# Causal attention and a gated expert layer on one core: port waits for GpSimd, a store moved ahead of a load, and new numbers in the planner

## The chip, the cores and the metric

The kernel runs on one core of a Trainium2 chip. The metric is the device time of one execution in microseconds (us). The kernel before was timed in three runs: 681.15, 683.09 and 684.12 us, median 683.09.

## What is computed

Four batches of twelve heads go through causal attention (448 tokens, head width 64); the heads' outputs are joined to a matrix x of 1792 tokens by 768, and x goes through a gated layer with float32 weights.

```python
scores = scale * np.matmul(q, k.transpose(0, 1, 3, 2))
scores = np.where(mask, -1000000000.0, scores)
scores = scores - np.max(scores, axis=-1, keepdims=True)
attn = np.exp(scores)
attn = attn / (np.sum(attn, axis=-1, keepdims=True) + 1e-09)
attn_out = np.matmul(attn, v)
...
x = np.ascontiguousarray(attn_out.transpose(0, 2, 1, 3)).reshape(B * S, H * D)
g = x @ w_gate
silu = g * (1.0 / (1.0 + np.exp(-g)))
val = x @ w_val
return (silu * val @ w_out)
```

## The kernel before, in words

**Stages.** One chunk is one batch, 448 tokens. For each chunk the kernel does the attention of six pairs of heads, and then the layer: 36 weight tiles of 128x768 (24 of gate and value, 12 of the output matrix). A float32 product is made of three matmuls on high and low parts (`mm3`, L885 to L887): 2592 matmuls of 128x448 in all, with `M` (gate and value) and `MO` (output) as their names in the rows. Attention runs one chunk ahead: while TensorE multiplies the weights of chunk c, the other engines make chunk c+1's scores (`S`, L512), row maxima (L563), exponentials (L575), normalised rows (L620 on ScalarE, L624 on GpSimd), transposes (`T`, L678 and L710) and products with the values (`O`, L752 and L783). So every stage fills TensorE with two kinds of work.

**Weights.** In chunk 0 a weight arrives as 64-bit numbers, 768 KB (`wide`, three buffers, load at L859). A copy takes the upper part into the single tile `top` (ScalarE, L317, or GpSimd, L323), a VectorE instruction joins it with the lower bits into float32 (`wraw`, two buffers, L868), and two more instructions split `wraw` into a high and a low part (`whl`, L317, L323, L339 or L342). `wraw` is also stored to HBM (`wr`, 384 KB, L832, the function `keep`), so that chunk 1 can load it back. A `wraw` buffer is free again when its split is done and its store has landed. In chunk 1 the split parts are stored (`ws`), and chunks 2 and 3 load them.

**Order.** A planner written in the kernel sets the order of everything. Each operation has costs per engine (`cost`, L65), a due time, dependencies and buffers; `Planner.run` gives out operations in time order, lets operations that can run on several engines choose one, and returns one list. The program is then written out in this list's order, and each engine runs its own instructions in that order. The planner knows that VectorE and GpSimd share a port to the on-chip memory: an operation marked `port` on VectorE and any operation on GpSimd never overlap in the plan (`lock`, `begin`). In the program nothing holds them to that: an engine starts an instruction when its semaphores allow it. All loads and stores go through one queue, issued by SyncE (SP) in plan order; a DMA whose semaphore is not there yet holds up all that are behind it.

**End.** The output tile of the last `MO` is scaled and moved to on-chip memory in two halves, 256 columns by ScalarE (L954) and 192 by VectorE (L955), each with a store of its own (L962). All other output tiles are one instruction of 448 columns and one store (L974).

Of the kernel before, what the change touches and what calls it, by code (L numbers as in the profile page):

```python
# [8 lines left out]
F32 = mybir.dt.float32  # L9
# [5 lines left out]
AF = mybir.ActivationFunctionType  # L15
ALU = mybir.AluOpType

P = 128
# [45 lines left out]

def cost(e, kind, n):  # L65
    if e == "ACT":
        return {"psum": 66, "sbuf": 110, "ptr": 190, "exp": 280, "tanh": 160}[kind] / 1e3 + n / 1200
    if e == "DVE":
        return 0.075 + n / {"one": 1920}.get(kind, 960)
    if e == "POOL":  # L70
        return {"one": 190, "ptr": 260, "two": 180}[kind] / 1e3 + n / {"two": 465.0}.get(kind, 1200.0)
    return {"r": max(n * 0.4475e-3 + 0.0025, 0.109), "f": n * 0.4475e-3 + 0.0045, "n": n / 600, "t": n * 0.109 / 128}[kind] + 0.001


class Res:
# [154 lines left out]
def kernel(  # L230
# [25 lines left out]
    def buf(shape, dt, tag, base, name):  # L256
        return pool.tile(shape, dt, tag=tag, name=name, bufs=CAPS[base])
# [46 lines left out]
    def op(alts, due, deps=(), alloc=(), uses=(), extra=0.0):  # L304
        first = [heads[r.tag] for r in alloc if r.tag in heads]
        o = pl_.op(alts, due, list(deps) + first, alloc, uses, extra)
        o.soft = first
        o.port = bool(alts.pop("port", False))
        o.kb = alts.pop("kb", 0)
        o.kind = alts.pop("kind", "m")  # L310
        for r in alloc:
            heads[r.tag] = o
        return o

    def copies(kind, n, out, in_, scale=1.0, engines="ADP"):
        def act():
            nc.scalar.activation(out(), in_(), AF.Copy, scale=scale)  # L317

        def dve():
            nc.vector.tensor_scalar(out(), in_(), scale, None, ALU.mult)  # L320

        def gps():
            nc.gpsimd.tensor_scalar(out(), in_(), scale, 1.0, ALU.mult, ALU.mult)  # L323

        r = {}
        if "A" in engines:
            r["ACT"] = (cost("ACT", kind, n), act)
        if "D" in engines:
            r["DVE"] = (cost("DVE", "one" if kind == "sbuf" else "two", n), dve)
        if kind == "sbuf":  # L330
            r["port"] = True
        if "P" in engines and kind == "sbuf":
            r["POOL"] = (cost("POOL", "one", n), gps)
        return r

# [476 lines left out]
    def weights(i):  # L812
        c, g = seq[i]
        due = start[c + 1] + LEN[c + 1] * g / NW
        w = wt[i] = {}
        rhl = Res("whl")

        def newhl():
            w["hl"] = buf([P, 2, WC], F32R, "whl", "whl", f"whl{i}")
            w["h"], w["l"] = w["hl"][:, 0], w["hl"][:, 1]  # L820

        def split(ra, rw):
            def newh():
                newhl()
                return w["h"]
            h = op(copies("sbuf", WC, newh, lambda: w["raw"]), due - 6 * WLEAD, [ra], [rhl], [rw])
            l = op(binary(WC, lambda: w["l"], lambda: w["raw"], lambda: raw(w["h"])), due - 5 * WLEAD, [h], [], [rw, rhl])
            wops[i] = (h, l, rhl, rhl)
            return h, l

        def keep(dst, src, deps, use, kb):
            return op({"SP": (0.3, lambda: nc.sync.dma_start(dst, src())), "kb": kb}, due - 3 * WLEAD, deps, [], [use])  # L832

        if c and (g, "hl") in stored:
            def load():
                newhl()
                nc.sync.dma_start(raw(w["hl"]), scratch[g])
            ld = op({"SP": (0.3, load), "kb": 768}, due - 10 * WLEAD, [stored[g, "hl"]], [rhl])
            wops[i] = (ld, ld, rhl, rhl)
            return  # L840
        if c:
            rw = Res("wraw")

            def load():
                w["raw"] = buf([P, WC], F32, "wraw", "wraw", f"wraw{i}")
                nc.sync.dma_start(w["raw"], scratch1[g])
            ld = op({"SP": (0.3, load), "kb": 384}, due - 12 * WLEAD, [stored[g, "raw"]], [rw])
            h, l = split(ld, rw)
            if c in RAW and c < NCHUNK - 1:
                stored[g, "hl"] = keep(scratch[g], lambda: raw(w["hl"]), [h, l], rhl, 768)  # L850
            return

        rw, r64, rt_ = Res("wraw"), Res("wide"), Res("top")

        def load():
            w["wide"] = buf([P, 4 * WC + 4], U16, "wide", "wide", f"wide{i}")
            nc.sync.dma_start(w["wide"][:, 1 : 4 * WC + 1], wP[g].bitcast(U16))  # L859
        ld = op({"SP": (0.3, load), "kb": 768}, due - 16 * WLEAD, alloc=[r64])  # L860

        def upper():
            return top.bitcast(F16).rearrange("p (n w) -> p n w", w=2)[:, :, 1]

        def lower():
            w["raw"] = buf([P, WC], F32, "wraw", "wraw", f"wraw{i}")
            z = w["wide"].bitcast(U32).rearrange("p (n w) -> p n w", w=2)[:, :WC, 1]
            nc.vector.scalar_tensor_tensor(w["raw"].bitcast(U32), z, 13, top, ALU.logical_shift_right, ALU.bitwise_or)  # L868

        bf = lambda: w["wide"].bitcast(BF16).rearrange("p (n w) -> p n w", w=4)[:, 1 : WC + 1, 0]  # L870
        g0 = op(copies("sbuf", WC, upper, bf), due - 10 * WLEAD, [ld], [rt_], [r64])
        ra = op({"DVE": (cost("DVE", "two", WC), lower), "port": True}, due - 8.5 * WLEAD, [g0], [rw], [r64, rt_])

        h, l = split(ra, rw)
        if 0 in RAW:
            stored[g, "hl"] = keep(scratch[g], lambda: raw(w["hl"]), [h, l], rhl, 768)
        else:
            stored[g, "raw"] = keep(scratch1[g], lambda: w["raw"], [ra], rw, 384)

    ps = {}  # L880

# [7 lines left out]
    def moe(c):  # L889
# [45 lines left out]
        for m in range(KD):  # L935
            rM = Res("M")
            prev = None
            for f in range(NF):
                half, kb = divmod(f, KD)
                gi = 2 * NF + 2 * m + half  # L940
                i = base + gi
                wh_, wl_, rwh, rwl = wops[i]
                a, l, rhh, rhl = h_ops[f]

                def mm(f=f, kb=kb, i=i, m=m):
                    if f == 0:
                        ps[c, "o", m] = bank("M", f"MO{c}_{m}")
                    mm3(ps[c, "o", m], i, kb, N, hh[f][:, :N], hl[f][:, :N], f == 0, f == NF - 1)
                prev = op({"PE": (m3, mm)}, at(gi + kb / KD), [prev, wh_, wl_, a, l],
                          [rM] if f == 0 else [], [rwh, rwl, rhh, rhl] + ([rM] if f else []))  # L950
            if (c, m) == (NCHUNK - 1, KD - 1):

                cut = 256
                for name, eng, put, a, b_ in (("ACT", nc.scalar, lambda o, i_: nc.scalar.activation(o, i_, AF.Copy, scale=0.5), 0, cut),  # L954
                                              ("DVE", nc.sync, lambda o, i_: nc.vector.tensor_scalar(o, i_, 0.5, None, ALU.mult), cut, N)):  # L955
                    ro = Res("osb")

                    def half(m=m, put=put, a=a, b_=b_):
                        o = ps[c, "s", m, a] = buf([P, T], F32, "osb", "osb", f"osb{c}_{m}_{a}")[:, a:b_]
                        put(o, ps[c, "o", m][:, a:b_])  # L960
                    e = op({name: (0.4, half)}, at(gi + 1) - BOOST, [prev], [ro], [rM])
                    op({"SP": (0.3, lambda m=m, eng=eng, a=a, b_=b_: eng.dma_start(  # L962
                        outT[m * P : (m + 1) * P, TO[c] + a : TO[c] + b_], ps[c, "s", m, a])), "kb": 112}, at(gi + 1), [e], [], [ro])
                continue
            ro = Res("osb")

            def newo(m=m):
                ps[c, "s", m] = buf([P, T], F32, "osb", "osb", f"osb{c}_{m}")[:, :N]
                return ps[c, "s", m]
            e = op(copies("psum", N, newo, lambda m=m: ps[c, "o", m][:, :N], 0.5, engines="AD"),  # L970
                   at(gi + 1) - BOOST, [prev], [ro], [rM])

            def store(m=m):
                nc.sync.dma_start(outT[m * P : (m + 1) * P, TO[c] : TO[c] + N], ps[c, "s", m])  # L974
            op({"SP": (0.3, store), "kb": 224}, at(gi + 1), [e], [], [ro])
# [3 lines left out]
    for c in range(NCHUNK):  # L979
# [4 lines left out]
            split_x(c, k)  # L984
        moe(c)
    order = pl_.run(CAPS)
    with tc.manual_schedule():
        for o in order:
            o.fn()


# [49 lines left out]
```

## Time and profile before

| | |
|---|---|
| runs | 681.15, 683.09, 684.12 us |
| profiled execution | 680.74 us; first to last instruction 678.9 us |
| TensorE busy | 667.2 us, 98% |
| VectorE busy | 378.3 us, 56% |
| ScalarE busy | 360.1 us, 53% |
| GpSimd busy | 218.5 us, 32% |
| DMA | 165.08 MB, 243 GB/s |

Busy time of TensorE is the union of its matmuls' modelled spans, which overlap; what it leaves is time in which no matmul ran. The granted clock was full in all 40 slices of the page.

### The profile page before, as it was taken

The numbers are of one execution on the slowest core, as the hardware profiler recorded it, in microseconds if no ns is written. First come the engines' busy times: TensorE is split into PE (matmuls) and PEld (weight loads), VectorE is DVE, ScalarE is ACT, GpSimd is POOL, SyncE is SP. The second block draws the span as 40 slices with busy tenths as digits, with TensorE's granted clock in tenths as the row PEclk, the third lists the DMA queues.
The fourth block names the chain that finished last, engine by engine and source line by source line (L and its number), as shares of the span: only waits on it lengthen the run. The fifth ranks groups of instructions, "written<-read, shape, count | busy, mean of one in ns | idle before, by whom it ended". The sixth has DMA issues, their size and how long they took to land.

```text
span 678.9 us, 10972 instructions
## 1 busy us (share of the span) xinstructions
PE 667.2 (98%) x3906; PEld 600.7 (88%) x3906; DVE 378.3 (56%) x926; ACT 360.1 (53%) x875; POOL 218.5 (32%) x256
## 2 busy tenths in 40 slices
PE   8999999999999999999999999999999999999997
PEld 5568899888999999999899999999999999999997
DVE  6778879797785676676765346545534222222100
ACT  7997688688683765654755345346354211111000
POOL 3773645456361342554423224224232000000000
PEclk9999999999999999999999999999999999999999
DMA  8868787878987978878688975554565666666671
GB/s 296 292 182 272 244 270 248 301 236 293 289 287 251 307 280 296 277 255 306 227 315 298 340 253 186 199 187 144 182 200 179 218 226 212 217 225 224 220 248 42
DMA packets 45446, 165.08 MB, mean 243 GB/s; under 512 B 5072, under 2 KB 14672, under 8 KB 45392
## 3 DMA queue, kind: packets, MB, share of 16 engines
q1 hardware_dynamic: 45088, 164.16, 72.2%
q8 instruction: 31, 0.51, 0.3%
q10 hardware_dynamic: 304, 0.23, 0.1%
q14 instruction: 23, 0.19, 0.1%
HBM read 116.39 MB, written 47.97 MB: 242 GB/s over the span
## 4 chain that ended last, share of the span: by engine, by line
PE 80%; DVE 6%; ACT 5%; DMA 5%; issue 2%; SPq 1%; POOL 1%; DVEq 0%; ACTq 0%; POOLq 0%
PE M L885 14%; PE M L886 14%; PE M L887 14%; PE MO L886 8%; PE MO L885 8%; PE MO L887 8%; PE S L512 5%; PE O L752 4%; DMA wr<-wraw 4%; PE T L710 4%; DVE wraw L868 3%; ACT p L575 2%; ACT p L620 1%; PE T L678 1%; PE O L783 1%
## 5 line engine op out<-in xcount | busy, mean ns | idle before, releaser
L885 PE MATMUL M<-xh,whl 128*128 128x448 f32 x576 | 215.4, 374 | 0.0
L886 PE MATMUL M<-xl,whl 128*128 128x448 f32 x576 | 209.4, 364 | 0.0
L887 PE MATMUL M<-xh,whl 128*128 128x448 f32 x576 | 209.1, 363 | 0.0
L887 PEld LDWEIGHTS M<-xh,whl 128*128 128x128 f32 x576 | 108.0, 188 | 7.7
L885 PEld LDWEIGHTS M<-xh,whl 128*128 128x128 f32 x576 | 108.2, 188 | 7.3 <-issue 0.3
L886 PEld LDWEIGHTS M<-xl,whl 128*128 128x128 f32 x576 | 108.4, 188 | 6.7 <-DVE xl L339 0.3
L885 PE MATMUL MO<-hh,whl 128*128 128x448 f32 x288 | 107.1, 372 | 0.0
L886 PE MATMUL MO<-hl,whl 128*128 128x448 f32 x288 | 104.6, 363 | 0.0
L887 PE MATMUL MO<-hh,whl 128*128 128x448 f32 x288 | 104.5, 363 | 0.0
L575 ACT ACTIVATE p<-p,m 128x192 f32<-128x192 f32 (+3 forms) x180 | 91.5, 513 | 3.3 <-DVE m L563 3.2
L563 DVE CUSTOM_DVE_ANT_0 p<-S,masks 128x192 f32<-128x192 f32 (+3 forms) x180 | 68.1, 426 | 16.9 <-PE S L512 16.4
L317 ACT ACTIVATE ph<-T 128x384 fp32r<-128x384 f32 (+3 forms) x95 | 47.5, 510 | 53.1 <-PE T L678 27.8
L339 DVE TENSOR_TENSOR whl<-wraw,whl 128x768 fp32r<-128x768 f32 x58 | 55.8, 962 | 10.0 <-ACT whl L317 8.0
L620 ACT ACTIVATE p<-p,rec 128x448 f32<-128x448 f32 (+3 forms) x130 | 58.7, 512 | 5.0 <-DVE rec L588 4.9
L317 ACT ACTIVATE hh<-t 128x448 fp32r<-128x448 f32 x42 | 24.1, 575 | 67.4 <-DVE t L928 67.4
L922 DVE SCALAR_TENSOR_TENSOR t<-t,M 128x448 f32<-128x448 f32 x48 | 29.7, 618 | 52.4 <-ACT t L918 52.3
L887 PEld LDWEIGHTS MO<-hh,whl 128*128 128x128 f32 x288 | 54.0, 188 | 3.8
L885 PEld LDWEIGHTS MO<-hh,whl 128*128 128x128 f32 x288 | 54.2, 188 | 3.4
L886 PEld LDWEIGHTS MO<-hl,whl 128*128 128x128 f32 x288 | 54.2, 188 | 3.2
L928 DVE TENSOR_TENSOR t<-t,M 128x448 f32<-128x448 f32 x48 | 29.6, 616 | 43.8 <-PE M L887 43.3
L339 DVE TENSOR_TENSOR pl<-T,ph 128x384 fp32r<-128x384 f32 x72 | 39.6, 549 | 23.0 <-ACT ph L317 22.7
L918 ACT ACTIVATE t<-M 128x448 f32<-128x448 f32 x48 | 26.0, 542 | 49.1 <-PE M L887 48.8
(82 smaller groups left out, 887.8 us busy)
## 6 DMA issues: line engine op xcount, KB each, us to landing
whl<-ws SPq DMA_DIRECT2D x72, 768.0 KB, 4.3
wide<-in_w_dram SPq DMA_DIRECT2D x36, 768.0 KB, 5.4
ws<-whl SPq DMA_DIRECT2D x36, 768.0 KB, 4.2
wr<-wraw SPq DMA_DIRECT2D x36, 384.0 KB, 5.9
wraw<-wr SPq DMA_DIRECT2D x36, 384.0 KB, 5.0
vraw<-in_v_dram SPq DMA_DIRECT2D x24, 256.0 KB, 4.4
qraw<-in_q_dram SPq DMA_DIRECT2D x23, 224.0 KB, 4.0
kraw<-in_k_dram SPq DMA_DIRECT2D x23, 224.0 KB, 4.7
```

Source lines behind the costliest of these rows:

```text
L317: nc.scalar.activation(out(), in_(), AF.Copy, scale=scale)
L339: r["DVE"] = (cost("DVE", "two", n), lambda: nc.vector.tensor_tensor(out(), a(), b(), alu))
L512: nc.tensor.matmul(st[u + y][f"S{i}"][:r], Q[:, q0 : q0 + r], K[:, :q1_] if y else K[:, S - q1_ :], start=z == 0, stop=z == len(passes) - 1)
L563: nc.vector.tensor_tensor_reduce(p[:r], s[f"S{i}"][:r], mask[:r, maskX - q0 : maskX - q0 + q1_] if h % 2 else back[:r, P - min(q1_, P) : P ...
L575: nc.scalar.activation(p[:r], p[:r], AF.Exp, bias=peak(i)[:r], scale=-1.0, accum_out=sums[u % NR][:r, i : i + 1],)
L620: nc.scalar.activation(p[:r], p[:r], AF.Copy, scale=rec[u % NR][:r, i : i + 1])
L710: nc.tensor.transpose(pt[:, o_ + q0 - bs : o_ + q0 - bs + r], s[f"p{i}"][:r, k0 : k0 + P], ident[:r, :r])
L885: nc.tensor.matmul(out[:, :n], a[:, w], xhi, start=first, stop=False)
L886: nc.tensor.matmul(out[:, :n], a[:, w], xlo, start=False, stop=False)
L887: nc.tensor.matmul(out[:, :n], l[:, w], xhi, start=False, stop=last)
L922: nc.vector.scalar_tensor_tensor(t, t, 1.0, ps[c, f, 0][:, :N], ALU.add, ALU.mult)
L928: nc.vector.tensor_tensor(t, t, ps[c, f, 1][:, :N], ALU.mult)
```

## The change

Five edits. (1) The planner's costs: the copy of `top` gets a kind of its own, `half`, with 340 instead of 110 ns of fixed cost on ScalarE, and a high-precision matmul loses some ns. (2) The store of `wraw` becomes due 17 instead of 3 units ahead of its weight's use, which is one unit ahead of a load. (3) The last output tile is no longer cut in two. (4) While the program is written out, the last VectorE operation marked `port` is kept; a GpSimd operation that comes after it in the plan, and starts there less than 4 us behind its end, gets a semaphore wait for it. (5) With the new costs the plan comes out in another order.

```diff
-        return {"psum": 66, "sbuf": 110, "ptr": 190, "exp": 280, "tanh": 160}[kind] / 1e3 + n / 1200
+        return {"psum": 66, "sbuf": 110, "half": 340, "ptr": 190, "exp": 280, "tanh": 160}[kind] / 1e3 + n / 1200
...
-    return {"r": max(n * 0.4475e-3 + 0.0025, 0.109), "f": n * 0.4475e-3 + 0.0045, "n": n / 600, "t": n * 0.109 / 128}[kind] + 0.001
+    return {"r": max(n * 0.4445e-3, 0.109), "f": n * 0.4475e-3 + 0.0045, "n": n / 600, "t": n * 0.109 / 128}[kind] + 0.001
...
-        def keep(dst, src, deps, use, kb):
-            return op({"SP": (0.3, lambda: nc.sync.dma_start(dst, src())), "kb": kb}, due - 3 * WLEAD, deps, [], [use])
+        def keep(dst, src, deps, use, kb, lead=3):
+            return op({"SP": (0.3, lambda: nc.sync.dma_start(dst, src())), "kb": kb}, due - lead * WLEAD, deps, [], [use])
...
-        g0 = op(copies("sbuf", WC, upper, bf), due - 10 * WLEAD, [ld], [rt_], [r64])
+        g0 = op(copies("half", WC, upper, bf), due - 10 * WLEAD, [ld], [rt_], [r64])
...
-            stored[g, "raw"] = keep(scratch1[g], lambda: w["raw"], [ra], rw, 384)
+            stored[g, "raw"] = keep(scratch1[g], lambda: w["raw"], [ra], rw, 384, 17)
...
-            if (c, m) == (NCHUNK - 1, KD - 1):
-
-                cut = 256
...
-                continue
...
+    after = mybir.DependencyInfo(mybir.DependencyClass.Sync, mybir.DependencyReason.DATA)
     with tc.manual_schedule():
+        port = None
         for o in order:
+            made = nc.cur_bb.bb.instructions
+            n = len(made)
             o.fn()
+            mine = [i for i in nc.cur_bb.bb.instructions[n:] if i.engine == {"DVE": nc.vector, "POOL": nc.gpsimd}.get(o.eng, nc.sync).engine]
+            if o.eng == "DVE" and o.port:
+                port = (o, mine[-1])
+            if o.eng == "POOL" and port and o.start - port[0].end < 4 and port[0] not in o.deps:
+
+                tc.add_manual_dep(mine[0], port[1].name, after, reason="port")
```

**The order it moves.** On SyncE's queue, in chunk 0's weights (the number behind `wide` and `wr` is the weight):

```order
-L859 DMA wide5_790<-in_w_dram 128x3072
 L832 DMA wr2_193<-wraw2_771 128x768
+L859 DMA wide5_791<-in_w_dram 128x3072
 L422 DMA vraw14_841<-in_v_dram 128x512
-L859 DMA wide6_858<-in_w_dram 128x3072
 L832 DMA wr3_194<-wraw3_847 128x768
-L859 DMA wide7_912<-in_w_dram 128x3072
+L859 DMA wide6_865<-in_w_dram 128x3072
 L832 DMA wr4_195<-wraw4_907 128x768
```

The load of weight 5 stood ahead of the store of weight 2 and now stands behind it; this pair, store of weight i and load of weight i+3, is turned round for all the weights of chunk 0 that have such a load.

On GpSimd, before, around the low part of weight 21 (`whl`, L342; `VS`, `QS` and `p` belong to attention, `hl` is the low part of a hidden tile):

```order
L323 TENSOR_SCALAR VS_1947<-vraw_1288 128x4x64 [waits DMAHW3_49,PE_49]
L342 TENSOR_TENSOR QS_1890<-qraw_1004,QS_1890 128x448 [waits DMAHW1_49,Activation_49]
L624 TENSOR_SCALAR p_3_1935<-p_3_1935,rec 128x448 [waits DVE_49,Activation_49]
L342 TENSOR_TENSOR VS_1947<-vraw_1288,VS_1947 128x4x64 [waits Pool_49]
L342 TENSOR_TENSOR whl_1913<-wraw_1888,whl_1913 128x768
L342 TENSOR_TENSOR hl_110<-t_9_1960,hh_98 128x448 [waits Activation_49]
```

and with the change:

```order
L342 TENSOR_TENSOR QS_1888<-qraw_1007,QS_1888 128x448 [waits DMAHW1_49,Activation_49]
L624 TENSOR_SCALAR p_0_1462<-p_0_1462,rec 64x64 [waits DVE_49,Activation_49]
L624 TENSOR_SCALAR p_2_1931<-p_2_1931,rec 128x320 [waits Activation_49]
L342 TENSOR_TENSOR KS_1902<-kraw_1033,KS_1902 128x448 [waits DMAHW2_49]
L342 TENSOR_TENSOR whl_1913<-wraw_1886,whl_1913 128x768 [waits DVE_49,Pool_49]
L323 TENSOR_SCALAR top<-wide_1905 128x768 [waits DMAHW1_49,DVE_49,Activation_49]
```

The same low part had no wait and followed its neighbour at once; now it waits for VectorE. Over the whole program GpSimd's rows that wait for VectorE go from 68 to 116. TensorE has the same 3764 rows, in the same order up to about its 297th, which is in the first products of chunk 0.

At the end, on ScalarE (`osb` is an output tile on its way out):

```order
-L954 ACTIVATE osb_5_0_7224<-MO_5_7184 128x256 [waits DMAHW1_49,PE_49,Activation_49]
-L962 DMA out_dram<-osb_5_0_7224 128x256 [waits DMAHW3_49,Activation_49]
-L1037 UNCONDITIONAL_BRANCH
+L317 ACTIVATE osb_5_7224<-MO_5_7184 128x448 [waits DMAHW1_49,PE_49,Activation_49]
+L1033 UNCONDITIONAL_BRANCH
```

One instruction of ScalarE takes the place of two halves, and one store of SyncE that of two.

## Rows read from the trace of the kernel before

**Rows 1.** The page: span and busy time of the engines.

```profile
span 678.9 us, 10972 instructions
PE 667.2 (98%) x3906; PEld 600.7 (88%) x3906; DVE 378.3 (56%) x926; ACT 360.1 (53%) x875; POOL 218.5 (32%) x256
```

**Rows 2.** Busy time by stretch: stretch, length, engines (x instructions), clock, DMA share, GB/s.

```profile
10.00:50.00 40.00, 38.46 (x280) 23.78 (x276) 31.45 (x113) 39.52 (x121) 26.79 (x31) 1.00 0.80 268
50.00:100.00 50.00, 49.09 (x298) 43.36 (x299) 40.71 (x88) 38.55 (x85) 27.04 (x25) 1.00 0.83 267
100.00:160.00 60.00, 57.35 (x336) 51.40 (x335) 52.20 (x102) 47.78 (x99) 29.75 (x30) 1.00 0.83 265
...
280.00:340.00 60.00, 59.47 (x351) 54.65 (x350) 41.48 (x95) 36.99 (x91) 25.25 (x27) 1.00 0.79 270
```

**Rows 3.** Timeline of TensorE: start, length, what [idle before, who ended it].

```profile
50.13 0.44 PE L678 MATMUL T<-ident,p 128*128 128x128 f32 x2 [0.73 <-POOL p L624]
...
75.49 0.65 PE L752 MATMUL O<-ph,VS 128*128 128x448 f32 x3 [0.56 <-DVE ph L339]
...
76.89 0.52 PE L710 MATMUL T<-ident,p 128*128 128x128 f32 x3 [0.22 <-DVE ph L339]
...
129.50 0.52 PE L710 MATMUL T<-ident,p 128*128 128x128 f32 x3 [0.21 <-DVE ph L339]
...
137.36 0.59 PE L752 MATMUL O<-pl,VS 128*72 128x128 f32 x3 [0.55 <-DVE pl L339]
...
145.93 0.52 PE L710 MATMUL T<-ident,p 128*128 128x128 f32 x3 [0.87 <-DVE rec L587]
...
157.44 0.64 PE L752 MATMUL O<-ph,VS 128*128 128x448 f32 x3 [0.88 <-DVE ph L339]
...
334.97 0.55 PE L710 MATMUL T<-ident,p 128*128 128x128 f32 x3 [0.53 <-DVE pl L339]
```

**Rows 4.** L868's instructions (ns min/median/max), then timelines of VectorE and GpSimd.

```profile
L868 DVE SCALAR_TENSOR_TENSOR wraw<-wide,top x36: 940/958/2803, 18.2 to 202.3; 128x768 uint32<-128x768 uint32 x36
...
70.26 1.84 POOL L342 TENSOR_TENSOR whl<-wraw,whl 128x768 fp32r<-128x768 f32 x1
70.78 2.13 DVE L868 SCALAR_TENSOR_TENSOR wraw<-wide,top 128x768 uint32<-128x768 uint32 x1
...
142.13 1.84 POOL L342 TENSOR_TENSOR whl<-wraw,whl 128x768 fp32r<-128x768 f32 x1
142.30 2.49 DVE L868 SCALAR_TENSOR_TENSOR wraw<-wide,top 128x768 uint32<-128x768 uint32 x1
...
330.52 2.80 DVE L339 TENSOR_TENSOR hl<-t,hh 128x448 fp32r<-128x448 f32 x1 [0.33 <-ACT hh L317]
331.15 1.15 POOL L342 TENSOR_TENSOR KS<-kraw,KS 128x448 fp32r<-128x448 f32 x1
332.28 0.56 POOL L323 TENSOR_SCALAR xh<-xs 128x448 fp32r<-128x448 f32 x1
```

**Rows 5.** Stores of L832: landing; and two links of the chain that ended last.

```profile
DMA to landing us min/median/max: 2.3/5.5/10.5
...
127.79 7.09 DMA wr<-wraw
...
149.84 5.82 DMA wr<-wraw
```

**Rows 6.** The end: timeline; landing of the two halves' stores (L962), of all others (L974).

```profile
668.26 0.55 ACT L317 ACTIVATE osb<-MO 128x448 f32<-128x448 f32 x1 [6.65 <-PE MO L887]
675.46 0.39 ACT L954 ACTIVATE osb<-MO 128x256 f32<-128x256 f32 x1 [6.65 <-PE MO L887]
675.88 0.36 DVE L955 TENSOR_SCALAR osb<-MO 128x192 f32<-128x192 f32 x1 [41.77 <-ACT osb L954]
...
DMA to landing us min/median/max: 1.6/1.7/1.7
...
DMA to landing us min/median/max: 2.0/4.6/9.2
```

More of the change, by code (lines that the diff above doesn't have):

```diff
@@ L328, in copies @@
         if "D" in engines:
-            r["DVE"] = (cost("DVE", "one" if kind == "sbuf" else "two", n), dve)
-        if kind == "sbuf":
+            r["DVE"] = (cost("DVE", "two" if kind == "psum" else "one", n), dve)
+        if kind != "psum":
             r["port"] = True
-        if "P" in engines and kind == "sbuf":
+        if "P" in engines and kind != "psum":
             r["POOL"] = (cost("POOL", "one", n), gps)
@@ L950, in moe @@
                           [rM] if f == 0 else [], [rwh, rwl, rhh, rhl] + ([rM] if f else []))
-            if (c, m) == (NCHUNK - 1, KD - 1):
-                cut = 256
[L954 to L963, printed above, removed]
-                continue
             ro = Res("osb")
```

## The prediction

> **What bounds the kernel now.** First the page: TensorE is busy for 667.2 of 678.9 us [rows 1]. No other engine is near that, so only time in which TensorE stands still, and the end after its last matmul, can be won; its own work stays, since the change leaves it the same 3764 rows. Second, busy time by stretch, which shows where it stands still: 40.00 - 38.46 = 1.54 us between 10 and 50 us, 0.91 between 50 and 100, 2.65 between 100 and 160, and 0.53 between 280 and 340 [rows 2]. That is 5.63 us, and nearly all that a new order can win. The reader is to see there too that between 10 and 50 us ScalarE works for 39.52 of 40 us, and that between 100 and 160 us, where TensorE loses most, VectorE is busy for 52.20 of 60 us and the DMA engines for 0.83 of the time: in the stretch in which chunk 0's weights are made, a late VectorE operation has little room to catch up.
>
> Third, TensorE's timeline, for who ended each of these waits [rows 3], and behind that the timelines of VectorE and GpSimd and the chain of waits [rows 4, 5]. They fall into three kinds.
>
> - **Held by the port.** L868's median is 958 ns, its longest 2803 [rows 4]. At 70.78 it takes 2.13 us. GpSimd had begun a 1.84 us instruction at 70.26, which ended at 72.10, and L868 ended 0.81 us later, at 72.91. At 142.30 it takes 2.49 us, and ends at 144.79, again 0.82 us behind the end of GpSimd's instruction (143.97) [rows 4]. VectorE did not work slowly there, it was kept out. What stood behind it in VectorE's order came late, and TensorE waited 0.56 and 0.22 us (75.49, 76.89), 0.87 (145.93), and 0.53 (334.97, behind the held L339 at 330.52) [rows 3]: 2.18 us.
> - **A `wraw` buffer not yet stored.** The chain shows two stores of 7.09 us from 127.79 and 5.82 us from 149.84, and then L868, which needs the buffer [rows 5]. Behind these lie the waits at 137.36 and 157.44, 0.55 and 0.88 us [rows 3]: 1.43 us. The wait of 0.21 us at 129.50 comes behind an L868 that was both late for its buffer and held.
> - **The rest**: 5.63 - 2.18 - 1.43 - 0.21 = 1.81 us, of which 0.73 at 50.13, where GpSimd's own operation was late [rows 3].
>
> **The change, part by part.** *GpSimd's waits.* 48 more of its rows wait for VectorE. They take away nothing by themselves; they put VectorE's operation first wherever the plan has it first. At weight 21, the very place of the L868 held at 142.30, the low part that held the port had no wait and now has one. I credit the whole 2.18 us, and half of the 0.21. What it costs: behind a waiting GpSimd instruction all of GpSimd's order stands, the normalised rows (which TensorE's transposes wait for) and the parts of Q, K and V. GpSimd is busy for 32% [rows 1], which is the cover. The price of one such delay that gets through is bounded from below by nothing and from above by the row at 50.13, 0.73 us [rows 3]. I take nothing for the forecast, since the plan already counts these gaps on GpSimd and has given them room, and keep the upper end for a rival.
>
> How much a held operation loses decides this term. At 330.52 VectorE is held until behind 332.84, while GpSimd runs one instruction behind another (331.15, 332.28) [rows 4]: the port did not come to VectorE between them. The Trainium skill says otherwise (SBUF — State Buffer, "Who interferes with whom"): the one that starts first has the shared ports for its whole instruction, and the second is blocked until that one ends. By that rule the hold would have been over by 332.30 at the latest, the 0.53 us would be no matter of the port, and the sum would be about 680.0. The row decides, and the term stays at 2.18.
>
> *The store ahead of the load.* Both wait for the same L868, so neither starts later for a wait; the store gets ahead of 768 KB. Its landing is 5.5 us at the median, 7.09 and 5.82 at the two places, and 2.3 at the least [rows 5]. With nothing new ahead of it, I expect it nearer the 2.3 than the 5.5, say 4: two to three us are saved per buffer, more than the 0.55 and 0.88 that TensorE lost, so I credit 1.43 us and the other half of the 0.21. The load lands later by the store's own issue and transfer, between nothing and 2.3 us. Two other `wide` buffers lie between a load and its use, and no wait of a weight's matmul is among TensorE's waits, so I count nothing; if that cover were gone, each weight would come up to 2.3 us late. The loads of Q, K and V behind the pair keep their place.
>
> *The end.* Before: ScalarE's half 0.39, then VectorE's half 0.36, one after the other (675.46, 675.88), then a store that lands 1.6 us after its issue: 675.46 to about 677.86. Now: one instruction of 0.55 us, as at 668.26, and one store of 224 KB, which lands in 2.0 us at the least and 4.6 at the median of a crowded queue [rows 6]. The queue is empty at the end, so I take 2.0: 0.55 + 0.03 + 2.0 = 2.58 against 2.40, so +0.2 us (bounds -0.2 with 1.6, +2.8 with 4.6).
>
> *The new costs and the new order.* The copy of `top` and the matmul's cost only move things. Nine high parts of weights go from ScalarE to GpSimd, six normalisations the other way; both sides are covered by idle time outside the first 50 us, and there the order is the same as before. From TensorE's 297th row on, every place is another one. I count nothing for it, bounded by the rest, 1.81 us, on the gaining side, and by the rivals on the other.
>
> **Sum.** 680.74 - 2.18 - 1.43 - 0.21 + 0.2 = 677.1 us for the profiled execution. This one was 2.35 us faster than the median of the three runs, 683.09, and I put the same difference on the median: 683.09 - 3.62 = **679.5 us**. Half a per cent, 3.4 us, is about what a measurement of this kernel can tell from no change; the forecast lies just beyond it, by 0.53%.
>
> **The rivals.**
>
> *The new order has waits of its own* (28%). The listed waits are the places where the old order went wrong; the new one has other places. For it: 2.35 us between two executions of one and the same program show that such waits come and go; a plan is right only as far as its costs are. Against it: the held operations are a thing that the plan never wanted. Time: 679.5 + 2.35 = 681.8, up to 684.5 where two such lots come.
>
> *The waits don't bite* (12%). Where the plan itself has GpSimd's operation first, no wait is added, and VectorE is held as before. For it: the holds at 70.78 and 142.30 begin only 0.52 and 0.17 us behind GpSimd's start, so a plan could well have had either first [rows 4]. Then 2.18 us and half of the 0.21 stay, and only the store counts: 683.09 - 1.43 - 0.1 + 0.2 = 681.8.
>
> *GpSimd becomes the late one* (13%). A wait is for a VectorE operation that may itself be late, and GpSimd, which could have run, stands; the normalised rows and the split Q and K behind it come late, and the transposes and scores wait in TensorE's order with all that follows. The place is chunk 0 and 1, 50 to 340 us, where most of GpSimd's work lies. Price: 0.73 us each, the row at 50.13 [rows 3]. To end 3.4 us above the time before, 7.0 us are needed beyond the forecast: ten of the 48 would have to get through. With twelve, 679.5 + 8.8 = 688.3 us. Against it: GpSimd's 32%, and that between 50 and 340 us only one of the eight listed waits was for it. The Trainium skill's summary on the same page (SBUF — State Buffer, "Summary: rules for kernel authors") advises to hold back whichever is off the critical path; nothing here shows yet that this is GpSimd at every one of the 48.
>
> **How the numbers follow.** The forecast has 47%: its own range, 676.5 to 680.7, lies for the greater part under 679.7 (40 points faster, 7 the same). The new order's own waits: 3 faster, 23 the same, 2 slower. Waits that don't bite: 2 and 10. GpSimd late: 3 the same, 10 slower. That makes 45% faster by over 0.5%, 43% within it, 12% slower. The range takes in the bounds: at the low end all 5.63 us gone and about half of the 2.35 too, 676.3; at the high end the second rival lot and the end's upper bound, 685.0.
>
> **What would show it.** Right: no L868 over about 1.2 us between 60 and 210 us, no wait of L868 for a store, stores of L832 landing in some 4 us, and TensorE's idle time between 50 and 160 us under 1.5 instead of 3.56 us. Wrong: L868 still at 2 us and more (the waits don't bite); TensorE waiting for GpSimd's L624 or for scores behind L342 (GpSimd late); weights' matmuls waiting for a load of `wide` (the store's cover gone); or as much idle time as before at new places.

## The result and the profile after

The changed kernel takes 675.3 us (median of five runs, 674.35 to 675.69), against 683.09 before; the ratio of the two is 0.9905, with a 95% interval of 0.9884 to 0.9927. It is faster, by 7.8 us between the medians and by 6.5 us (0.95%) by the ratio, which sets the runs of both side by side. The forecast was 679.5 us, 3.6 us faster: the right sign, about half the size. The median lies 1.0 us below the low end of the range; 683.09 times the ratio, 676.6, lies just inside it.

The page of the changed kernel, its groups in the order of the page:

```profile
span 672.5 us, 11031 instructions
...
PE 666.1 (99%) x3906; PEld 601.9 (89%) x3906; DVE 373.0 (55%) x924; ACT 357.4 (53%) x877; POOL 210.5 (31%) x255
...
wide<-in_w_dram SPq DMA_DIRECT2D x36, 768.0 KB, 6.6
...
wr<-wraw SPq DMA_DIRECT2D x36, 384.0 KB, 3.5
```

The same two groups on the page of the kernel before (KB each, median us from issue to landing):

```profile
wide<-in_w_dram SPq DMA_DIRECT2D x36, 768.0 KB, 5.4
...
wr<-wraw SPq DMA_DIRECT2D x36, 384.0 KB, 5.9
```

The changed kernel's busy time by stretch, in the columns of [rows 2]:

```profile
10.00:50.00 40.00, 38.71 (x280) 23.75 (x276) 30.73 (x113) 40.00 (x123) 27.43 (x33) 1.00 0.78 275
50.00:100.00 50.00, 49.73 (x305) 44.81 (x306) 41.88 (x92) 41.13 (x92) 21.59 (x23) 1.00 0.83 285
100.00:160.00 60.00, 60.00 (x374) 55.33 (x373) 50.67 (x104) 48.61 (x104) 27.95 (x29) 1.00 0.80 281
...
280.00:340.00 60.00, 60.00 (x358) 55.27 (x357) 39.78 (x92) 35.57 (x86) 25.78 (x29) 1.00 0.79 272
```

All that TensorE waited for in the changed kernel (who, for whom: us in total, times, longest):

```profile
PE warm L283 <- DVE xs L278: 1.0, 1, 1.0
PE T L678 <- POOL p L624: 0.7, 1, 0.7
PE O L783 <- ACT ph L317: 0.7, 1, 0.7
PE S L509 <- DMA kraw<-in_k_dram: 0.2, 1, 0.2
PE T L710 <- ACT ph L317: 0.2, 1, 0.2
```

And the instructions of L868, as in [rows 4]:

```profile
L868 DVE SCALAR_TENSOR_TENSOR wraw<-wide,top x36: 943/953/1603, 18.3 to 193.0; 128x768 uint32<-128x768 uint32 x36
```

The reader is to see three things. TensorE has no wait left behind 51 us: between 100 and 160 us it is busy for all of 60 us, where it was busy for 57.35 [rows 2]. (That 374 matmuls stand in this stretch instead of 336 is mostly the new order: 24 of the 38 more are short ones of `S`.) L868 no longer takes 2.8 us, but 1.6 at the most. And the stores of raw weights land in 3.5 us at the median (5.9 on the page before), while the loads behind them land later, in 6.6 (5.4 before); no matmul of a weight waits for that.

### The profile page after: what moved, and what is told of

Its sections match the earlier page's. It is cut to its first block, busy times and chain, and to the rows that moved or that the text cites. A ratio compares the mean times of both kernels' runs of the same rounds, so it can differ in the third digit from the quotient of the medians.

```text
span 672.5 us, 11031 instructions
## 1 busy us (share of the span) xinstructions
PE 666.1 (99%) x3906; PEld 601.9 (89%) x3906; DVE 373.0 (55%) x924; ACT 357.4 (53%) x877; POOL 210.5 (31%) x255
## 4 chain that ended last, share of the span: by engine, by line
PE 95%; ACT 3%; DMA 0%; DVE 0%; issue 0%; POOL 0%; ACTq 0%; DVEq 0%
PE M L885 17%; PE M L886 17%; PE M L887 17%; PE MO L885 9%; PE MO L886 9%; PE MO L887 9%; PE S L512 6%; PE O L752 5%; PE T L710 4%; PE O L783 1%; PE T L678 1%; ACT p L575 1%; ACT p L620 1%; DMA kraw<-in_k_dram 0%; POOL p L624 0%
## 5 line engine op out<-in xcount | busy, mean ns | idle before, releaser
L620 ACT ACTIVATE p<-p,rec 128x320 f32<-128x320 f32 (+3 forms) x136 | 59.9, 501 | 4.5 <-DVE rec L588 4.5
L339 DVE TENSOR_TENSOR whl<-wraw,whl 128x768 fp32r<-128x768 f32 x58 | 57.6, 993 | 7.1 <-ACT whl L317 5.9
L339 DVE TENSOR_TENSOR pl<-T,ph 128x384 fp32r<-128x384 f32 x72 | 39.6, 550 | 18.0 <-ACT ph L317 17.3
```

Of the source, the lines that this page charges most:

```text
L339: r["DVE"] = (cost("DVE", "two", n), lambda: nc.vector.tensor_tensor(out(), a(), b(), alu))
L620: nc.scalar.activation(p[:r], p[:r], AF.Copy, scale=rec[u % NR][:r, i : i + 1])
```

## The experiments

Twelve experiments ran, on ten kernels, each timed in several runs beside the kernel before on the same chip. They fall into three lots of four; each lot had a chip of its own, on which the kernel before took 680.53, 681.37 and 680.60 us. So the ratios are compared, and medians only inside a lot.

### The parts one by one, in the old order

The change mixes a new order with everything else. The first three kernels keep the order of before and add single parts; the fourth is the whole change without its waits.

`w_only`: the kernel before, with the loop that writes out the program taken from the change.

```diff
         for o in order:
+            made = nc.cur_bb.bb.instructions
+            n = len(made)
             o.fn()
...
+            if o.eng == "POOL" and port and o.start - port[0].end < 4 and port[0] not in o.deps:
+                tc.add_manual_dep(mine[0], port[1].name, after, reason="port")
```

> The order of before, word for word, with GpSimd's added waits alone. Port theory (VectorE held out by GpSimd makes most of the waits that went): 2.5 to 3.3 us faster than before, L868 nowhere over 1.7 us. Order theory (the new plan with its better costs did it, the waits are idle): within 1 us of before. Store theory: the same, within 1 us, with the waits at 137 and 157 us still there.

675.58 us, ratio 0.9928 (0.9910 to 0.9946): 4.9 us faster, more than any theory said. L868 is at 1704 ns at the longest. All that TensorE waited for behind 51 us in this kernel:

```profile
PE T L710 <- DVE ph L339: 1.9, 2, 1.7
PE O L752 <- DVE ph L339: 0.2, 1, 0.2
```

So the waits at 137 and 157 us, which the prediction gave to the store, are gone too, although the stores land in 6.4 us here, no earlier than before. But one wait is new, from the timeline of VectorE and TensorE:

```profile
102.06 0.96 DVE L868 SCALAR_TENSOR_TENSOR wraw<-wide,top 128x768 uint32<-128x768 uint32 x1 [2.11 <-DMA wr<-wraw]
...
104.69 0.52 PE L710 MATMUL T<-ident,p 128*128 128x128 f32 x3 [1.75 <-DVE ph L339]
```

With the port free, VectorE waits 2.11 us for a store before L868: L868 waited 7.2 us in seven places for stores here, where it had waited 3.6 in five before. That VectorE reaches L868 earlier, and that the second fault had been hiding in part behind the first, would explain this; it is argued and not shown. The profiled execution was the slowest of the six (677.34 us), 1.8 us above the median, so the new wait need not be in the others.

`swap_only`: the old order, in which each store of a raw weight changes places with the load just ahead of it.

```diff
     order = pl_.run(CAPS)
+    sp = [i for i, o in enumerate(order) if o.eng == "SP"]
+    for i, j in zip(sp, sp[1:]):
+        if order[i].kb == 768 and order[j].kb == 384 and len(order[j].deps) and order[j].deps[0].eng == "DVE":
+            order[i], order[j] = order[j], order[i]
```

> The order of before, with each store of a raw weight put ahead of the load that stood just ahead of it, and nothing else. Store theory: 1.5 to 2.1 us faster than before, the waits at 137 and 157 us gone, the stores landing in some 3.5 instead of 5.9 us. Port theory and order theory: within 0.7 us of before, though the stores land earlier.

678.45 us, ratio 0.9967 (0.9956 to 0.9979): 2.1 us faster, as the store theory said. The stores land in 3.0 us, L868 waits for none, and the wait that stood at 137 us is gone; that at 157 has shrunk to 0.35 us. The waits at 75 us (0.56) and before 335 us (0.53) stay exactly as in [rows 3]: they were not the store's. But the wait at 145.93, which the prediction gave to the port alone, has shrunk from 0.87 to 0.33 us, although L868 is held for 2.49 us ahead of it as before.

`w_swap`: both of these edits together.

> The order of before with both, the waits and the store ahead of the load. If port and store are all of it: 5 to 6.5 us faster than before, as the whole change. If the plan's new order had a share of its own: 2 to 4 us faster only.

675.03 us, ratio 0.9919 (0.9903 to 0.9935): 5.5 us faster. Its profiled span is 672.5 us, that of the whole change, and past 51 us one wait of 0.2 us is left. The old order with the port and the store settled is as good, to what these runs can tell, as the new one. 4.9 and 2.1 add up to 7.0 and not to 5.5: some of the waits fall to either edit, that at 137 us wholly, those at 145 and 157 in great part.

`no_wait`: the whole change, with the old two-line loop in place of the waits.

> The whole change without the added waits: new costs, new order, store ahead, whole last tile. Port theory: 2.5 to 3.5 us slower than the whole change, with L868 of 2 us and more again. Order theory: within 1 us of the whole change, so 6 to 7 us faster than before.

675.87 us, ratio 0.9928 (0.9912 to 0.9945): about a quarter of a per cent behind the whole change, less than the port theory said and more than the order theory (the intervals of the two ratios overlap). In the trace what is lost stands in one place. Without the waits, from VectorE's and GpSimd's timeline and TensorE's:

```profile
138.55 1.16 POOL L342 TENSOR_TENSOR KS<-kraw,KS 128x448 fp32r<-128x448 f32 x1
...
138.96 3.36 DVE L868 SCALAR_TENSOR_TENSOR wraw<-wide,top 128x768 uint32<-128x768 uint32 x1
...
139.67 1.84 POOL L342 TENSOR_TENSOR whl<-wraw,whl 128x768 fp32r<-128x768 f32 x1
...
143.47 0.52 PE L710 MATMUL T<-ident,p 128*128 128x128 f32 x3 [1.07 <-DVE rec L587]
```

The same instructions in the whole change, which has the same order:

```profile
137.96 1.16 POOL L342 TENSOR_TENSOR KS<-kraw,KS 128x448 fp32r<-128x448 f32 x1
...
140.08 1.87 POOL L342 TENSOR_TENSOR whl<-wraw,whl 128x768 fp32r<-128x768 f32 x1 [0.96 <-DVE wraw L868]
...
138.37 1.58 DVE L868 SCALAR_TENSOR_TENSOR wraw<-wide,top 128x768 uint32<-128x768 uint32 x1
```

This is the mechanism in one picture. GpSimd holds the port with one instruction (`KS`) when L868 comes. Without the wait the next one (`whl`) follows at once, L868 is let in behind both and takes 3.36 us, and TensorE waits 1.07. With the wait GpSimd pauses 0.96 us, L868 takes 1.58, and TensorE does not wait. Not every hold costs something: three other L868 of `no_wait` take 1.86, 1.97 and 2.46 us (at 90.94, 116.67 and 194.89), and TensorE waits behind none of them.

### The new costs, and the store inside the new order

`whole` is the change again, for a comparison on one chip.

> The whole change again, beside the next three on one chip. All theories: 6 to 7 us faster than before, as first measured.

674.53 us, ratio 0.9901 (0.9885 to 0.9917): as first measured.

`costs_only`: the kernel before with the planner's new costs alone (the two lines of `cost`, and `half` in `copies` and for `top`).

> Before with the planner's new costs alone, so a new order, with no added wait, the store's old due time and the halved end. If the new order brings nothing of its own: within 1 us of before. If it places the work better, as the version without the waits hints: 2 to 4 us faster than before.

678.86 us, ratio 0.9963 (0.9951 to 0.9976): 2.5 us faster, so the order theory's forecast. But not for want of faults: L868 still takes up to 2133 ns, the stores land in 6.1 us, and TensorE has waits at new places, the longest 1.47 us at 154.94. L868 waits for a store in one place here (2.3 us) and not in five; why this order loses less is not shown.

`no_store`: the whole change with the store's due time of before.

```diff
-            stored[g, "raw"] = keep(scratch1[g], lambda: w["raw"], [ra], rw, 384, 17)
+            stored[g, "raw"] = keep(scratch1[g], lambda: w["raw"], [ra], rw, 384)
```

> The whole change with the store's old due time, behind the load; the planner orders anew. Store theory, with its share on top of the waits as small as the fixed order showed it (0.6 us): 0.3 to 1 us slower than the whole change. If store and waits add up instead: 1.7 to 2.2 us slower. L868 waits for stores again, some 7 us in all.

676.14 us, ratio 0.9925 (0.9910 to 0.9939), 1.6 us behind the whole change: just under the sum's 1.7 to 2.2, and above the small 0.3 to 1. L868 waits 6.9 us in six places for stores, which land in 7.2 us at the median. (The due time also moves the plan, so this holds the new order's difference too.)

`no_costs`, in the third lot: the whole change with the old costs.

> The whole change with the planner's old costs; store's new due time, waits and the whole last tile stay. If the costs do nothing once port and store are settled: within 0.7 us of the whole change. If they carry the better order: 1.5 us or more slower.

675.07 us, ratio 0.9915 (0.9894 to 0.9936), beside 675.08 for the whole change in the same lot. Once port and store are settled the costs do nothing that can be measured. That the order theory was right for `costs_only` and wrong here is no contradiction: an order matters as long as it can be broken.

### Waits both ways

The whole change holds GpSimd to the plan, but not VectorE. `mirror` adds the other direction:

```diff
             if o.eng == "DVE" and o.port:
                 port = (o, mine[-1])
+                if pool_ and o.start - pool_[0].end < 4 and pool_[0] not in o.deps:
+                    tc.add_manual_dep(mine[0], pool_[1].name, after, reason="port")
+            if o.eng == "POOL":
+                pool_ = (o, mine[-1])
```

> The whole change, and the mirror of its waits: a VectorE port operation also waits for the GpSimd operation that the plan has ahead of it by less than 4 us. If the plan's order at the port is right both ways: 0.5 to 1 us faster than the whole change, with the wait of TensorE at 50 us shorter. Rival: VectorE, the busier of the two, is now held where GpSimd is late, 1 to 4 us slower.

673.91 us, ratio 0.9894 (0.9875 to 0.9913), 0.6 us below the whole change in its lot. L868 now takes 946 to 960 ns in all its 36 places. What it changes for TensorE is the wait at 50 us. In the whole change (the run `whole`), from three engines' timelines:

```profile
47.55 1.08 POOL L323 TENSOR_SCALAR top<-wide 128x768 f16<-128x768 bf16 x1 [2.33 <-DVE rec L587]
48.13 0.92 DVE L339 TENSOR_TENSOR xl<-xs,xh 128x448 fp32r<-128x448 f32 x1 [0.39 <-ACT xh L317]
...
48.58 1.66 POOL L624 TENSOR_SCALAR p<-p,rec 128x320 f32<-128x320 f32 x1
...
48.97 0.94 DVE L339 TENSOR_TENSOR whl<-wraw,whl 128x768 fp32r<-128x768 f32 x1
...
50.29 0.44 PE L678 MATMUL T<-ident,p 128*128 128x128 f32 x2 [0.73 <-POOL p L624]
```

and with waits both ways:

```profile
48.41 0.54 POOL L624 TENSOR_SCALAR p<-p,rec 128x320 f32<-128x320 f32 x1
...
48.98 0.62 DVE L339 TENSOR_TENSOR xl<-xs,xh 128x448 fp32r<-128x448 f32 x1 [1.40 <-POOL p L624]
```

GpSimd's normalised row, which TensorE needs, had been held behind two instructions of VectorE; now VectorE, which has time there, is the one that waits.

The third lot repeats this, beside the old order and old costs with the store moved and waits both ways (`w_swap_mirror`):

> The old order and old costs with the store ahead of the load and waits both ways at the port. If the new order adds nothing once port and store are settled: level with the next version, within 1 us, some 7 us faster than before. If the new order is worth something by itself: 1.5 us or more slower than the next version.

> The whole change with waits both ways, again, beside the old order with the same waits. Some 7 us faster than before; both theories differ only in how far the version above is from it.

> The whole change on the same chip, for the worth of the mirrored waits: 0.5 to 1 us slower than the version with waits both ways if the wait at 50 us is all that they take away; level with it if that wait is given back later.

674.71 us for the old order with all waits (ratio 0.9910), 674.28 for the new order with them (0.9906), 675.08 for the change as it stands (0.9917). The old order is level with the new one. Waits both ways were 0.6 and 0.8 us faster than the whole change in two lots, on which the trace's 0.6 us less idle time at 50 us agrees, but the intervals of the ratios overlap: the gain is shown in the trace and not by the times.

## Why the prediction was right, and where it was short

**The two causes were the right ones.** Held by the port: L868's hold at 142.30 [rows 4] has its like in `no_wait`, at 138.96, and shrinks from 3.36 to 1.58 us with the wait alone. A buffer not yet stored: `swap_only` takes away the wait at 137 us and most of that at 157. The old order with both is level with the whole change within the intervals, so these two are all that the runs can tell.

**The sum was short in its terms, because idle time is short.** It took each wait of TensorE as the idle time that the timeline prints, 3.82 us in seven waits. A matmul's span here is 0.36 us while the next starts 0.20 us behind it, so the first 0.16 us of every wait lies under the span of the matmul before it. In the trace of before, around the wait of 0.87 us at 145.93 [rows 3]:

```profile
144.50 0.36 PE L886 MATMUL M<-xl,whl 128*128 128x448 f32 x1
144.70 0.36 PE L887 MATMUL M<-xh,whl 128*128 128x448 f32 x1
```

From 144.70 to 145.93 are 1.23 us where 0.20 is usual: 1.03 lost, not 0.87. Counted so, from start to start, the seven waits are worth 0.72, 0.38, 0.38, 0.71, 1.03, 1.03 and 0.69: 4.94 us. Three more, shorter than that or just above it (at 101.25, 103.60 and 360.25: 0.14, 0.30 and 0.30), were in no row of the prediction and are gone too: 5.68. The span fell by 678.9 - 672.5 = 6.4 us, although the end is 0.1 us longer and the work behind the wait at 50 us starts 0.14 later: some 1.0 us more, which no single row shows and which stay untraced.

**The rest was taken for lasting.** Of the 1.81 us that no term explained, the prediction kept all. In the same four stretches of the changed kernel 1.29 + 0.27 + 0 + 0 = 1.56 us are left, 1.40 of them in the two waits at 42 and 50 us (0.66 and 0.74), so this was right but for 0.25.

**The 2.35 us between the profiled execution and the median** were carried over. Here the medians fell 7.8 us where the spans of the profiled executions fell 6.4, and the five runs now lie within 1.3 us, where the kernel before had 3.0. It may be that waits of the same kinds come and go between executions, as the first rival said, and that the change took these away too; no slower execution of the kernel before was profiled, so this is not shown. In the three lots the kernel before had medians of 680.5 to 681.4 us, near the profiled 680.74, and in the two of them that have the whole change it was 6.8 and 5.5 us faster. So part of the 7.8 may be that 683.09 was a slow median, and what the sum missed is some 2 to 3 us.

**How port and store share it.** The prediction gave 2.29 to the port and 1.54 to the store. Alone they are worth 4.9 and 2.1 us, together 5.5. So the store is worth 0.6 us on top of the waits in the old order (the intervals overlap), and 1.6 in the new (`no_store`). The port's term was the one sized too small: it took only the waits whose last link was a held instruction, and `w_only` takes away those at 137 and 157 as well. The split by the last link was wrong, since these waits needed both causes. That a held L868 also sends its store and the work behind it late would explain it; no run shows that by itself.

**The store's cover held.** Landing was expected at about 4 us, and is 3.5. (The median of 5.5 in [rows 5] is that of all 72 stores of L832, half of them `ws`, of 768 KB; the raw weights' own was 5.9.) The loads got 1.2 us later, inside the bounds of nothing to 2.3, and no matmul waits for one. **The end** was priced at +0.2 us: from the start of the last instruction of ScalarE to the end of the span it was 678.9 - 675.46 = 3.44 us [rows 6], and is 3.55 (668.95 to 672.5), so +0.1; no run takes it alone. **The first 50 us** stay nearly as they were: TensorE is busy for 38.71 us from 10 to 50, where it was 38.46 [rows 2]. **One sign of being right failed**: four L868 between 60 and 210 us take over 1.2 us, the longest 1.6; TensorE waits behind none of them. The other three signs came.

**Two slips of sum.** Two lots of 2.35 us above 679.5 make 684.2, not 684.5, and the terms named for the range's high end do not make 685.0; the result lies at the other end.

**The rivals.** GpSimd late fell: GpSimd does wait now, and the only wait of TensorE for it is the one at 50 us, which stood there before. The Trainium skill (SBUF — State Buffer, "Summary: rules for kernel authors") says of such a pair: "Schedule whichever is off the critical path". If that means to hold this one back, the rows agree: at 138 us it is GpSimd, at 48 us VectorE. Waits that don't bite: in part, L868 still comes to 1.6 us where GpSimd has the port when it arrives. TensorE does not wait behind these holds; the 0.6 us that `mirror` adds are the wait at 50 us, where VectorE held GpSimd. A new order with its own waits: the new order has them (`costs_only`), but not once the two causes are gone.

## What to carry to other kernels

Where one engine is busy nearly all the time, look through its few waits for a common cause, and follow each back past its last link to the instruction that took longer than its like; here one instruction of 0.95 us that sometimes took 2.8 led to most of them. Measure a wait from start to start, not by the printed idle time, where the bound engine's instructions overlap. And where a static order assumes that two engines do not collide, a semaphore wait at the places where they may can be cheap beside what a collision costs, as it was here; the order itself then hardly mattered.

## What the runs showed of the hardware that was not expected

The port between VectorE and GpSimd is not always handed over between two instructions that follow one another without a pause. In `no_wait`, L868 comes at 138.96 under `KS`, which ends at 139.71; the next, `whl`, ends at 141.51, and L868 at 142.32, 0.81 us behind it, as at both holds of [rows 4]. The Trainium skill (SBUF — State Buffer, "Who interferes with whom") has the second blocked until the first instruction ends; by that L868 would have ended at about 140.52 (an estimate, 139.71 + 0.81), 1.8 us earlier, and the measurement decides. The held L339 at 330.52 [rows 4] is another such place.

Elsewhere the port did change hands at once, and there the rows agree with the page. From GpSimd's and VectorE's timelines of the kernel before:

```profile
119.40 1.16 POOL L342 TENSOR_TENSOR hl<-t,hh 128x448 fp32r<-128x448 f32 x1
120.51 1.46 POOL L342 TENSOR_TENSOR VS<-vraw,VS 128x256 fp32r<-128x256 f32 x1
...
120.22 1.15 DVE L339 TENSOR_TENSOR whl<-wraw,whl 128x768 fp32r<-128x768 f32 x1
```

VectorE comes under the first, which ends at 120.56, and is done 0.81 us behind it, while the second, which followed without a pause, still runs until 121.97. So it is at 48 us of `whole`: `xl`, begun at 48.13 under the copy of `top` (until 48.63), is done at 49.05, long before GpSimd's row, which was there at 48.58. That row is then held behind `xl` and behind the `whl` that follows it without a pause (until 49.91): it takes 1.66 us instead of 0.54, so here VectorE kept the port from one instruction to the next. What decides between the two cases no run shows. A pause of the holder was enough where the change makes one: behind GpSimd's pause of 0.96 us in the whole change L868 ends at 139.95, 0.83 us behind `KS`.
